# Sizes' low words, a flag asked for early, and loads planned to land later in a fused attention and expert kernel

## The chip, the cores and the metric

The kernel runs on one core of one Trainium2 chip. The metric is the device time of one execution in microseconds (us), as the median of several runs. An execution can also be profiled; the profile covers the span from the core's first to its last instruction, and the device time is a little more than that span.

## What is computed

The reference chains three layers over 1,536 tokens (2 batches of 768), with 512 features:

```python
# attention: 8 heads of 64, window n_local=96 back, first n_global=8 keys always seen, ALiBi-like bias
scores = q @ k.T / 8 - slope[h] * dist;  scores[~keep] = -1e9
a = exp(scores - max);  a = a / (sum(a) + 1e-9);  x = a @ v
# layer 2: 4 experts of width 1024, dense, mixed by normalised domain_probs
p = domain_probs / (domain_probs.sum(-1) + 1e-9)
x = sum_e p[:, e] * (relu(x @ w1[e]) @ w2[e])
# layer 3: width 2048, h * clip(h + 3, 0, 6) / 6
h = x @ w_in;  out = (h * clip(h + 3, 0, 6) / 6) @ w_out
```

`n_global` and `n_local` arrive as 64-bit integers; `w_in` and `w_out` arrive as 64-bit floats, and the kernel converts them to 32 bits itself.

## The kernel before, in words

**Two bodies.** `body(True)` is the fast path, for a window of at most 96 and at most 8 global keys. After it the kernel computes a flag from the sizes (lines 1192 to 1198), every engine loads it into a register (`values_load`, line 1199), and `body(False)`, a general path, follows under `tc.If` (line 1200). With the inputs used here the flag is 1 and all engines jump over the second body.

**Sizes.** Each 64-bit size is read as two 32-bit words. DVE casts the words (line 179), joins low and high word into one float (lines 180 to 183), and builds from it the bias table `base`: the window part (lines 184, 186), minus four times the local size (`nl4`, line 185), the global columns (line 187), the first block's table (line 188) and the global columns of the window table (line 189). The tile `fast_c` that these read is the second load on SP's queue (line 162).

**Attention.** There are 24 pairs: one pair is two heads by 256 query tokens (two blocks `qb` of 128). For each pair (`plan_pair`, line 312) PE makes scores (line 351), DVE adds the bias and finds the maximum (line 366), ACT takes the exponential and its sum (line 381), DVE adds 1e-9 and inverts the sums of both blocks in one piece (`sums`, lines 391 to 393), POOL normalises (line 401), PE transposes (line 420), ACT copies one block and DVE the other out of PSUM (lines 442 and 437), PE multiplies by the values (line 457), and ACT copies the result to `xf` (line 467). Each pair's queries and keys come by one load (line 323) and its values by another (line 330).

**Gate.** `plan_gate` (line 572) loads `domain_probs` (line 586), normalises them on DVE in nine small instructions (lines 578 to 584) and stores them to DRAM (line 589). `plan_p` (line 1107) loads each expert's row back, spread over all partitions (line 1113); the DVE product at line 984 needs it.

**Layers 2 and 3.** Forty-eight steps run over batch, expert (or layer 3) and pairs of 128-wide slices. `plan_first` makes the first product by a seven-product Strassen scheme (lines 909, 913, 916), `plan_second` the second (lines 1088, 1091, 1092). All are split into a high and a low part, so three matmuls stand for one. `plan_convert` turns the 64-bit weights into 32-bit ones in 32 rounds of seven DVE instructions and stores them to DRAM (line 747), from where line 775 reads them back for layer 3. The final step of each batch copies the output from PSUM (`finish`, line 1117) and sends it out in eight transfers (line 1146); the last two of the whole kernel (`d == KC - 1`) leave from ACT's queue, the others from SP's.

**What sets the order.** The body is not written in the order in which it is issued. Each piece of work is handed to `Plan.add` with an engine ("load" stands for SP's queue), a cost, the pieces it follows and a rank. `Plan.emit` (line 90) then plays the pieces through in its own clock: an engine that is free takes, of the pieces that are ready, the one with the lowest rank; if only a high-ranked piece is ready, it takes that one at once. A piece is ready when the pieces before it have ended, plus a lag: nothing on the same engine, `LOAD` = 2.0 behind a load on another engine, `LATENCY` = 0.25 otherwise (line 138). The order that comes out is fixed; on the chip every engine works through its own queue in that order. PE's gaps in that clock are filled with idle matmuls (line 263). Attention pair `i` has ranks near `2 * i`, layers 2 and 3 have ranks from 200 up, copies and activations that free PSUM have negative ones, and conversions 100,000 and more.

Of the kernel before, what the change touches and what calls it, by code (L numbers as in the profile page):

```python
# [17 lines left out]
ALU = mybir.AluOpType  # L18
# [3 lines left out]
P = 128  # L22
# [6 lines left out]
KC = DM // P  # L29
# [29 lines left out]
class Plan:  # L59
# [7 lines left out]
    LOAD = 2.0  # L67
# [22 lines left out]
    def emit(self):  # L90
# [16 lines left out]
        while count < n:  # L107
# [38 lines left out]
def moe_attention_kernel(ctx, tc, qk, vw, sizes, dpt, w1, w2, w_in, w_out, ident_d, fast_d, slow_d, out):  # L146
# [29 lines left out]
    ng, nl, nl4 = nv[:, 0:1], nv[:, 1:2], nv[:, 6:7]  # L176
    flag = const.tile([P, 1], I32, name="flag")
    with tc.manual_schedule(engines={mybir.EngineType.DVE}):
        nc.vector.tensor_copy(nf[:], ni[:])
        nc.vector.scalar_tensor_tensor(out=nv[:, 2:4], in0=lo, scalar=0.0, in1=hi, op0=ALU.is_lt, op1=ALU.add)  # L180
        nc.vector.scalar_tensor_tensor(
            out=nv[:, 0:2], in0=nv[:, 2:4], scalar=4294967296.0, in1=lo, op0=ALU.mult, op1=ALU.add
        )
        nc.vector.tensor_scalar(out=window, in0=rel, scalar1=nl, scalar2=NONE, op0=ALU.is_ge, op1=ALU.mult)
        nc.vector.tensor_scalar(out=nl4, in0=nl, scalar1=-4.0, scalar2=None, op0=ALU.mult)
        nc.vector.scalar_tensor_tensor(out=window, in0=rel, scalar=-4.0, in1=window, op0=ALU.mult, op1=ALU.add)
        nc.vector.tensor_scalar(out=gidx, in0=gidx, scalar1=ng, scalar2=NONE, op0=ALU.is_ge, op1=ALU.mult)
        nc.vector.scalar_tensor_tensor(out=first, in0=gidx, scalar=nl4, in1=window[:, FAR:], op0=ALU.add, op1=ALU.max)
        nc.vector.scalar_tensor_tensor(
            out=global_keys, in0=gidx[:, :NG], scalar=nl4, in1=global_keys, op0=ALU.add, op1=ALU.max  # L190
        )
# [22 lines left out]
    def t_mm(n, count):  # L214
        return count * (0.0145 + n / 2400.0)

# [4 lines left out]
    def pools(bx, fast):  # L221
# [70 lines left out]
        def plan_bias(tabs, normalised):  # L292

            made = plan.add("dve", 1.9, lambda: None, (), -2.0)
            for h in range(H):
                for kind in range(2):
                    if h == 0:
                        started[h, kind] = made
                        continue

                    def scaled(h=h, kind=kind):
# [7 lines left out]
                        "pool", 0.46 if kind else 0.3, scaled, [made, normalised[3 * (h // 2) - 3] if h > 1 else None], (h // 2 * CPB - 2) * CH + 0.1 * h + 0.5 * kind  # L309
                    )  # L310

        def plan_pair(i, c, hp, tabs, place_users, normalised, biased, outs, x_bank):
# [78 lines left out]
            def sums():  # L391
                nc.vector.tensor_scalar(out=m["sm"][:], in0=m["sm"][:], scalar1=1e-9, scalar2=None, op0=ALU.add)
                nc.vector.reciprocal(m["sm"][:], m["sm"][:])

            r = plan.add("dve", 0.4, sums, weighed, rank)
            normal = []
            for qb in range(CH):
                for j in range(2):
# [7 lines left out]
                    normal.append(plan.add("pool", 0.46 if kinds[qb] else 0.32, normalise, [r], rank))  # L406
# [793 lines left out]
    with tc.If(is_fast == 0):  # L1200
        body(False)
# [71 lines left out]
```

## Time and profile before

| | us |
|---|---|
| median of 3 runs (lowest to highest) | 848.62 (847.82 to 850.08) |
| the profiled execution | 847.26 |
| span of that execution | 845.2 |
| PE busy | 833.7 |
| DVE busy | 655.2 |
| ACT busy | 402.0 |
| POOL busy | 68.1 |

How to read it: the profiled execution took 847.26 us, of which 845.2 us are the span in which the profile sees instructions. PE is TensorE's matmuls, PEld its weight loads, DVE VectorE, ACT ScalarE, POOL GpSimd, SP SyncE. A letter q behind an engine's name means its sequencer or DMA queue. "L1146" is line 1146 of the kernel before. The granted clock of TensorE was 1.00 in all stages. A busy share near the full span says that an engine could be the bound; which wait ends last in a stage says whether it is.

### The profile page before, as it was taken

What the parts mean: (1) busy time and instruction counts of PE and PEld (TensorE: products, weight loads), DVE (VectorE), ACT (ScalarE), POOL (GpSimd) and SP (SyncE); (2) the same over time, 40 slices, a digit from 0 to 9 for tenths busy, and PEclk for the clock granted to TensorE, in tenths of its full rate; (3) what the DMA queues carried; (4) which work ended last, traced back from release to release, by engine and by line L of the source; (5) the groups of instructions that cost most, each with busy time, mean ns of one, the idle gap of its engine ahead of it and who ended that gap; (6) DMA issues with size and microseconds to landing.
All of it is one profiled execution on the core that took longest, in us unless ns stands there. A gap on an engine that the chain in (4) does not pass through costs nothing.

```text
span 845.2 us, 13646 instructions
## 1 busy us (share of the span) xinstructions
PE 833.7 (99%) x5090; PEld 763.2 (90%) x5090; DVE 655.2 (78%) x1366; ACT 402.0 (48%) x850; POOL 68.1 (8%) x131
## 2 busy tenths in 40 slices
PE   8999999999999999999999999999999999999997
PEld 6777999999999999999999999999999999999996
DVE  6999989988998977987777688689898766545442
ACT  6998643543433433543333333335666455545441
POOL 5888200000000000000000000000000000000000
PEclk9999999999999999999999999999999999999999
DMA  7873454465565565645656664744452555534302
GB/s 264 314 221 94 175 202 153 138 211 181 166 209 194 165 222 180 204 150 179 216 172 199 208 208 158 234 165 140 174 163 103 172 186 185 190 125 139 136 1 79
DMA packets 56985, 147.34 MB, mean 174 GB/s; under 512 B 6480, under 2 KB 7760, under 8 KB 56912
## 3 DMA queue, kind: packets, MB, share of 16 engines
q1 hardware_dynamic: 56480, 145.69, 52.2%
q8 instruction: 42, 0.69, 0.3%
q10 hardware_dynamic: 432, 0.71, 0.3%
q14 instruction: 31, 0.25, 0.1%
HBM read 109.66 MB, written 36.72 MB: 173 GB/s over the span
## 4 chain that ended last, share of the span: by engine, by line
PE 92%; DMA 3%; DVE 2%; POOL 1%; ACT 1%; issue 0%; SPq 0%; POOLq 0%; DVEq 0%; ACTq 0%
PE o L1091 16%; PE o L1092 15%; PE o L1088 15%; PE x_x L909 8%; PE x_x L913 8%; PE x_x L916 8%; PE w_w L913 6%; PE w_w L916 6%; PE w_w L909 6%; PE att_q L420 2%; PE att_q L351 1%; PE att_q L457 1%; DMA qkraw<-in_qk 1%; DMA w<-qkraw 1%; POOL t L401 1%; PE att_x L457 1%
## 5 line engine op out<-in xcount | busy, mean ns | idle before, releaser
L1091 PE MATMUL o<-hh,w2l 128*128 128x512 f32 (+1 forms) x768 | 259.4, 338 | 0.0
L1092 PE MATMUL o<-hl,w2h 128*128 128x512 f32 (+1 forms) x768 | 259.0, 337 | 0.0
L1088 PE MATMUL o<-hh,w2h 128*128 128x512 f32 (+1 forms) x768 | 257.8, 336 | 0.0
L933 ACT COPY snap<-x_x 128x384 f32<-128x384 f32 x144 | 68.9, 478 | 195.9 <-PE x_x L916 195.7
L946 DVE TENSOR_TENSOR c_c<-w_w,snap 128x384 f32<-128x384 f32 x144 | 80.0, 556 | 104.4 <-ACT w2h L250 58.5
L1092 PEld LDWEIGHTS o<-hl,w2h 128*128 128x128 f32 x768 | 144.4, 188 | 16.0
L1088 PEld LDWEIGHTS o<-hh,w2h 128*128 128x128 f32 x768 | 144.4, 188 | 13.4
L1091 PEld LDWEIGHTS o<-hh,w2l 128*128 128x128 f32 x768 | 144.5, 188 | 12.7
L909 PE MATMUL x_x<-xoh,w1h 128*128 128x384 f32 x384 | 129.7, 338 | 0.1
L916 PE MATMUL x_x<-xoh,w1l 128*128 128x384 f32 x384 | 129.0, 336 | 0.0
L913 PE MATMUL x_x<-xol,w1h 128*128 128x384 f32 x384 | 128.9, 336 | 0.0
L913 PE MATMUL w_w<-xol,w1h 128*128 128x384 f32 x288 | 97.1, 337 | 0.0
L909 PE MATMUL w_w<-xoh,w1h 128*128 128x384 f32 x288 | 97.0, 337 | 0.0
L916 PE MATMUL w_w<-xoh,w1l 128*128 128x384 f32 x288 | 96.8, 336 | 0.0
L250 ACT CAST w2h<-wr 128x1024 fp32r<-128x1024 f32 x48 | 50.4, 1050 | 61.2 <-PE o L1092 59.1
L909 PEld LDWEIGHTS x_x<-xoh,w1h 128*128 128x128 f32 x384 | 72.3, 188 | 3.2 <-issue 0.6
L913 PEld LDWEIGHTS x_x<-xol,w1h 128*128 128x128 f32 x384 | 72.3, 188 | 2.0
L1015 ACT CAST hh<-c_c 128x384 fp32r<-128x384 f32 x96 | 49.4, 514 | 48.3 <-DVE c_c L984 47.8
L916 PEld LDWEIGHTS x_x<-xoh,w1l 128*128 128x128 f32 x384 | 72.0, 188 | 0.0
L250 ACT CAST w1h<-wr 128x512 fp32r<-128x512 f32 x96 | 46.9, 510 | 49.5 <-PE w_w L913 45.7
L255 DVE TENSOR_TENSOR w2l<-wr,w2h 128x1024 fp32r<-128x1024 f32 x48 | 58.5, 1219 | 2.3 <-ACT w2h L250 2.3
L984 DVE SCALAR_TENSOR_TENSOR c_c<-c_c,p 128x384 f32<-128x384 f32 x96 | 53.8, 561 | 3.2
(90 smaller groups left out, 1132.7 us busy)
## 6 DMA issues: line engine op xcount, KB each, us to landing
wr<-in_w SPq DMA_DIRECT2D x64, 512.0 KB, 3.9
wr<-w SPq DMA_DIRECT2D x32, 512.0 KB, 3.5
kept<-w1h SPq DMA_DIRECT2D x24, 512.0 KB, 3.0
kept<-w1l SPq DMA_DIRECT2D x24, 512.0 KB, 4.8
w1h<-kept SPq DMA_DIRECT2D x24, 512.0 KB, 3.7
w1l<-kept SPq DMA_DIRECT2D x24, 512.0 KB, 4.9
qkraw<-in_w_in SPq DMA_DIRECT2D x16, 512.0 KB, 4.3
w<-qkraw SPq DMA_DIRECT2D x32, 256.0 KB, 4.2
```

What stands on the lines that cost most here:

```text
L250: nc.scalar.copy(out_ap, src)
L255: nc.vector.tensor_tensor(out_ap, src, hi_ap.bitcast(F32), op=ALU.subtract)
L909: nc.tensor.matmul(ps_, wh[:, a, cols], xh[:, o, kc, :], start=start and kc == 0, stop=False, skip_group_check=True,)
L913: nc.tensor.matmul(ps_, wh[:, a, cols], xl[:, o, kc, :], start=False, stop=False, skip_group_check=True)
L916: nc.tensor.matmul(ps_, wl[:, a, cols], xh[:, o, kc, :], start=False, stop=last, skip_group_check=True)
L933: nc.scalar.copy(m["n", n][:], m["x"][:, :HT])
L946: nc.vector.tensor_tensor(m[name][:], m["w"][:, :HT], m["n", n][:], op=ALU.add)
L984: nc.vector.scalar_tensor_tensor(out=room_for(), in0=src(), scalar=0.0, in1=p["p"][:, cols], op0=ALU.max, op1=ALU.mult)
L1015: nc.scalar.copy(at(0), room_for())
L1088: nc.tensor.matmul(o, wh, hh, start=first and own and f == 0, stop=False, skip_group_check=True)
L1091: nc.tensor.matmul(o, wl, hh, start=False, stop=False, skip_group_check=True)
L1092: nc.tensor.matmul(o, wh, hl, start=False, stop=end, skip_group_check=True)
```

## The change

The sizes' low words alone now feed the bias table, and `nl4` moves to ScalarE; joining the words moves, with the flag, to a planned DVE piece `ask` of rank 100 behind batch 1's attention. The flag then also tests the lower side of `n_global`. The global columns of the window table become a planned piece of their own (`with_global`). Pair 0's sums are split by block. In the planner a load's result is now 2.0 away from whatever follows, another load too (`LANDING`; before, nothing was added from load to load), and a load that follows other work is 0.3 away (before 0.25). The gate's ranks rise from 9, 12, 13 to 18, 30, 31; the first row load's from 20 to 34, the second's from -1 to 100. All engines load the flag behind the first output copy of the last batch, and only the very last output transfer, not the last two, leaves from ACT's queue.

```diff
-    LOAD = 2.0
+    LOAD = 0.3
+    LANDING = 2.0
...
-                lag = 0.0 if other == engine else self.LOAD if engine == "load" else self.LATENCY
+                if other == engine != "load":
+                    lag = 0.0
+                else:
+                    lag = self.LANDING if engine == "load" else self.LOAD if other == "load" else self.LATENCY
...
+    ng_low, nl_low = nf[:, 0, 0:1], nf[:, 1, 0:1]
         nc.vector.tensor_copy(nf[:], ni[:])
-        nc.vector.scalar_tensor_tensor(out=nv[:, 2:4], in0=lo, scalar=0.0, in1=hi, op0=ALU.is_lt, op1=ALU.add)
-        nc.vector.scalar_tensor_tensor(
-            out=nv[:, 0:2], in0=nv[:, 2:4], scalar=4294967296.0, in1=lo, op0=ALU.mult, op1=ALU.add
-        )
-        nc.vector.tensor_scalar(out=window, in0=rel, scalar1=nl, scalar2=NONE, op0=ALU.is_ge, op1=ALU.mult)
-        nc.vector.tensor_scalar(out=nl4, in0=nl, scalar1=-4.0, scalar2=None, op0=ALU.mult)
+        nc.scalar.mul(nl4, nl_low, -4.0)
+        nc.vector.tensor_scalar(out=window, in0=rel, scalar1=nl_low, scalar2=NONE, op0=ALU.is_ge, op1=ALU.mult)
...
-            made = plan.add("dve", 1.9, lambda: None, (), -2.0)
+            made = plan.add("dve", 0.9, lambda: None, (), -2.0)
+            whole = plan.add("dve", 0.22, with_global, [made], 0.0)
...
-            r = plan.add("dve", 0.4, sums, weighed, rank)
+            parts = [slice(qb, qb + 1) for qb in range(CH)] if i == 0 else [slice(0, CH)]
+            summed = [
+                plan.add("dve", 0.4, lambda part=part: sums(part), weighed[2 * part.start : 2 * part.stop], rank)
+                for part in parts
+            ]
...
-                    normal.append(plan.add("pool", 0.46 if kinds[qb] else 0.32, normalise, [r], rank))
+                    normal.append(plan.add("pool", 0.46 if kinds[qb] else 0.32, normalise, [summed[qb if i == 0 else 0]], rank))
...
-            a = plan.add("load", 0.2, lambda: nc.sync.dma_start(g[:], dpt.rearrange("e (p n) -> p e n", p=P)), (), 9)
-            b = plan.add("dve", 1.4, gate, [a], 12)
+            a = plan.add("load", 0.2, lambda: nc.sync.dma_start(g[:], dpt.rearrange("e (p n) -> p e n", p=P)), (), 18)
+            b = plan.add("dve", 1.4, gate, [a], 30)
             return plan.add(
-                "load", 0.2, lambda: nc.sync.dma_start(p_dram[:].rearrange("e (p n) -> p e n", p=P), g[:]), [b], 13
+                "load", 0.2, lambda: nc.sync.dma_start(p_dram[:].rearrange("e (p n) -> p e n", p=P), g[:]), [b], 31
             )
...
-                gates[b, g] = (t, plan.add("load", 1.0, load, wait + [gate], 20.0 if b == g == 0 else -1.0), p_users)
+                gates[b, g] = (t, plan.add("load", 1.0, load, wait + [gate], 34.0 if b == g == 0 else 100.0 if b == 0 and g == 1 else -1.0), p_users)
...
+                        if last and b == B - 1 and d == part == 0:
+                            plan.add(
+                                "act", 0.6, lambda: is_fast.append(nc.values_load(flag[0:1, 0:1], min_val=0, max_val=1)),
+                                [e], -9.0,
+                            )
...
-                            end = b == B - 1 and d == KC - 1
+                            end = b == B - 1 and d == KC - 1 and part == 1
...
+                plan.add("dve", 1.2, ask, x_ready[1], 100.0)
...
-    nc.vector.tensor_scalar(out=nv[:, 4:5], in0=nl, scalar1=1.0, scalar2=None, op0=ALU.is_ge)
...
-    is_fast = nc.values_load(flag[0:1, 0:1], min_val=0, max_val=1)
-    with tc.If(is_fast == 0):
+    with tc.If(is_fast[0] == 0):
         body(False)
```

`ask` holds six DVE instructions: the two that join the words, and four that make the flag.

## Rows read from the trace of the kernel before

**Rows 1.** The page: PE's busy time, and the chain that ended last by engine.

```profile
PE 833.7 (99%) x5090; PEld 763.2 (90%) x5090; DVE 655.2 (78%) x1366; ACT 402.0 (48%) x850; POOL 68.1 (8%) x131
...
PE 92%; DMA 3%; DVE 2%; POOL 1%; ACT 1%; issue 0%; SPq 0%; POOLq 0%; DVEq 0%; ACTq 0%
```

**Rows 2.** Stages: us, busy time of PE, PEld, DVE, ACT, POOL, PEclk, DMA share, GB/s.

```profile
20.00:40.00 20.00, 18.59 (x194) 13.98 (x192) 18.21 (x76) 18.37 (x65) 16.32 (x34) 1.00 0.87 305
...
96.00:400.00 304.00, 304.00 (x1738) 283.64 (x1739) 264.93 (x482) 125.37 (x223) 0.00 (x0) 1.00 0.56 182
...
700.00:839.00 139.00, 138.76 (x793) 128.46 (x791) 69.37 (x127) 65.20 (x121) 0.00 (x0) 1.00 0.37 126
```

**Rows 3.** Timeline, PE from 20 us: matmuls that began after idle time.

```profile
20.83 0.66 PE L457 MATMUL att_x<-at,v 104*64 104x128 f32 x8 [0.52 <-DVE at L437]
22.25 1.37 PE L351 MATMUL att_q<-qkraw 64*128 64x232 f32 x8 [0.18 <-DVE mn L366]
37.45 0.89 PE L351 MATMUL att_q<-qkraw 64*128 64x128 f32 x8 [0.70 <-DMA qkraw<-in_qk]
62.30 0.63 PE L420 MATMUL att_q<-qkraw,t 128*128 128x128 f32 x4 [1.22 <-DVE at L437]
```

**Rows 4.** Timeline of the tail: DVE's last copy.

```profile
838.92 0.42 DVE L1132 COPY xf<-o 128x256 f32<-128x256 f32 x1 [1.67 <-PE o L1092]
```

**Rows 5.** Lines 747, 1146, 1199, 1200: ns min/median/max, first and last start in us.

```profile
L747 SPq DMA_DIRECT2D w<-qkraw x32: 319/326/459, 123.6 to 688.3; - x32
...
L1146 ACTq DMA_DIRECT2D out_t<-xf x2: 351/822/1294, 838.8 to 839.4; - x2
...
L1199 PEldq TENSOR_LOAD <-flag x1: 758/758/758, 837.3 to 837.3; - x1
...
L1200 SPq EVENT_SEMAPHORE  x8: 17/17/17, 840.4 to 842.8; - x8
...
L1200 SPq COMPARE_BRANCH  x1: 53/53/53, 837.7 to 837.7; - x1
...
L1200 ACTq COMPARE_BRANCH  x1: 54/54/54, 841.3 to 841.3; - x1
...
L1200 ACTq EVENT_SEMAPHORE  x1: 17/17/17, 844.0 to 844.0; - x1
```

**Rows 6.** DMA issues: KB each, median us from issue to landing.

```profile
out_t<-xf SPq DMA_DIRECT2D x7, 128.0 KB, 1.9
...
p<-p_dram SPq DMA_DIRECT2D x8, 384.0 KB, 4.8
...
out_t<-xf ACTq DMA_DIRECT2D x1, 128.0 KB, 3.2
...
p_dram<-gate SPq DMA_DIRECT2D x1, 24.0 KB, 2.6
```

**Rows 7.** Timeline of the first 24 us: the table, pair 0, and the gate.

```profile
5.42 0.34 DVE L184 TENSOR_SCALAR base<-qkraw,nv 128x232 f32<-128x232 f32 x1
...
9.13 0.17 DVE L392 TENSOR_SCALAR sm<-sm 128x4 f32<-128x4 f32 x1 [0.99 <-ACT t L381]
...
10.12 1.66 PE L420 MATMUL att_q<-qkraw,t 128*128 128x128 f32 x6 [0.46 <-POOL t L401]
...
18.06 0.37 DVE L578 TENSOR_TENSOR gate_sum<-gate 128x12 f32<-128x12 f32 x1 [0.38 <-DMA gate<-in_dpt]
...
20.09 0.68 DVE L437 COPY at<-att_q 128x512 f32<-128x512 f32 x1
```

**Rows 8.** The chain that ended last, in order of time: three of its transfers.

```profile
1.20 4.20 DMA qkraw<-in_fast
...
28.63 8.68 DMA qkraw<-in_qk
...
688.33 5.50 DMA w<-qkraw
```

**Rows 9.** Waits of SP's queue: us in total, times, longest.

```profile
SPq L1113 <- DMA p_dram<-gate: 2.1, 1, 2.1
```

More of the change, by code (lines that the diff above doesn't have):

```diff
@@ L215, in t_mm @@
         return count * (0.0145 + n / 2400.0)
+    is_fast = []
     def body(fast):
@@ L292, in plan_bias, with with_global @@
         def plan_bias(tabs, normalised):
-            made = plan.add("dve", 1.9, lambda: None, (), -2.0)
+            made = plan.add("dve", 0.9, lambda: None, (), -2.0)
+            def with_global():
+                nc.vector.scalar_tensor_tensor(
+                    out=global_keys, in0=gidx[:, :NG], scalar=nl4, in1=global_keys, op0=ALU.add, op1=ALU.max
+                )
+            whole = plan.add("dve", 0.22, with_global, [made], 0.0)
             for h in range(H):
@@ L297, in plan_bias @@
                     if h == 0:
-                        started[h, kind] = made
+                        started[h, kind] = whole if kind else made
                         continue
@@ L308, in plan_bias @@
                     started[h, kind] = plan.add(
-                        "pool", 0.46 if kind else 0.3, scaled, [made, normalised[3 * (h // 2) - 3] if h > 1 else None], (h // 2 * CPB - 2) * CH + 0.1 * h + 0.5 * kind
+                        "pool", 0.46 if kind else 0.3, scaled, [whole if kind else made, normalised[3 * (h // 2) - 3] if h > 1 else None], (h // 2 * CPB - 2) * CH + 0.1 * h + 0.5 * kind
                     )
@@ L389, in plan_pair, with sums @@
                     )
-            def sums():
-                nc.vector.tensor_scalar(out=m["sm"][:], in0=m["sm"][:], scalar1=1e-9, scalar2=None, op0=ALU.add)
-                nc.vector.reciprocal(m["sm"][:], m["sm"][:])
-            r = plan.add("dve", 0.4, sums, weighed, rank)
+            def sums(part):
+                sm = m["sm"][:, part].rearrange("p a b -> p (a b)")
+                nc.vector.tensor_scalar(out=sm, in0=sm, scalar1=1e-9, scalar2=None, op0=ALU.add)
+                nc.vector.reciprocal(sm, sm)
+            parts = [slice(qb, qb + 1) for qb in range(CH)] if i == 0 else [slice(0, CH)]
[3 more added lines that the diff above has]
+            ]
             normal = []
@@ L1149, in finish, with ask @@
                 results[b] = done
+            if fast:
+                def ask():
+                    nc.vector.scalar_tensor_tensor(
+                        out=nv[:, 2:4], in0=lo, scalar=0.0, in1=hi, op0=ALU.is_lt, op1=ALU.add
+                    )
+                    nc.vector.scalar_tensor_tensor(
+                        out=nv[:, 0:2], in0=nv[:, 2:4], scalar=4294967296.0, in1=lo, op0=ALU.mult, op1=ALU.add
+                    )
+                    nc.vector.tensor_scalar(out=nv[:, 4:5], in0=nl, scalar1=1.0, scalar2=None, op0=ALU.is_ge)
+                    nc.vector.scalar_tensor_tensor(
+                        out=nv[:, 5:6], in0=nl, scalar=float(NPREV + 1), in1=nv[:, 4:5], op0=ALU.is_le, op1=ALU.mult
+                    )
+                    nc.vector.scalar_tensor_tensor(
+                        out=nv[:, 5:6], in0=ng, scalar=-2147483648.0, in1=nv[:, 5:6], op0=ALU.is_ge, op1=ALU.mult
+                    )
+                    nc.vector.scalar_tensor_tensor(
+                        out=flag[:], in0=ng, scalar=float(NG), in1=nv[:, 5:6], op0=ALU.is_le, op1=ALU.mult
+                    )
+                plan.add("dve", 1.2, ask, x_ready[1], 100.0)
             results = {}
```

12 lines of the change are left out of this document (2 added, 10 removed).

## The prediction, made before the change was run

> **What bounds the kernel now.** I read the page first: PE is busy for 833.7 of 845.2 us, and 92% of the chain that ended last is PE [rows 1]. Busy alone would not prove a bound, so the busy time by stage comes next: from 96 to 400 us PE is busy for 304.00 of 304 us, DVE for 264.93 [rows 2]. Layers 2 and 3 give nothing back unless matmuls go, and none do. What can move is PE's idle time: at the start, in the attention stage, and behind the last matmul. The timeline of PE from 20 us shows the attention gaps: 0.52, 0.18, 0.70 and 1.22 us [rows 3]; before them lies one of 0.46 us at 10.12 [rows 7]. In the tail DVE's last copy ends at 838.92 + 0.42 = 839.34 [rows 4], but the span ends at 845.2: 5.9 us in which no engine computes. The upper bound of the whole change is thus small: 3.1 us of gaps and a part of the tail.
>
> **The tail: -1.0 us (bounds -0.5 and -1.1).** ACT issues the last two outputs. The first issue takes 351 ns, the second 1,294 ns from 839.4, so until 840.7. Then ACT loads the flag, branches at 841.3, and its next instruction comes at 844.0, which is 2.7 us behind the branch [rows 5]. The span ends 1.2 us later. After the change the flag is in the register long before, and ACT issues one output instead of two. If that takes 0.35 us, ACT branches at 839.4 + 0.4 = 839.8 and is there at 842.5, 1.5 us earlier. But SP is then last. It now issues the second-to-last output, at 838.8 for about 0.35 us, branches at 839.2, and by its own row needs 840.4 - 837.7 = 2.7 us for the jump [rows 5]: 841.9. It then walks through eight waits on transfers and as many on engines. The last three of the first eight run from the landing of the last output, 839.4 + 3.2 = 842.6 [rows 6], to 842.8 [rows 5], so about 0.07 us each; sixteen make 1.1 us, and SP is through at 843.0 where ACT was at 844.0. Hence -1.0. If the single issue still takes 1.3 us, ACT arrives at 843.4 and only 0.5 us is gained; if SP's waits overlap more, 1.1. Here the rows weigh against a rule: a 128 KB output lands in 1.9 us from SP and in 3.2 us from ACT [rows 6], so which queue issues seems to matter.
>
> The Trainium skill, "DMA: Bandwidth & Descriptors", section "Issuing engines are not separate DMA queues", says that transfers from either engine run on the same 16 DMA engines, and that issuing from several saves sequencer time alone. By it the queue that issues makes no difference to the landing, the tail would give 0.5 us, and the sum would be -1.7. The trace's 1.9 against 3.2 us speak against it, with one transfer of this size on ACT to judge by.
>
> **The flag loads themselves: 0 (0 to +0.8).** All five engines now load the flag behind the first output copy, in the middle of the last matmuls. PE's load took 758 ns from 837.3, while PE's matmuls went on until 838.9, when DVE's copy, which waited for them, began [rows 4, 5]. PE's sequencer thus runs more than 0.76 us ahead, and the load hides there; without that lead the 0.76 us would be paid whole. On SP the load sits ahead of the first outputs, on ACT between copies; neither is late until the end. SP had loaded the flag early before and does so no longer; what it had to send then was waiting for scores anyway: 0.
>
> **The table: 0 (0 to -0.2).** Two small joins leave DVE's chain, but line 184 began at 5.42 [rows 7], right behind the landing of `fast_c` at 1.20 + 4.20 = 5.40 [rows 8]. The removed work was hidden behind that load. The product for `nl4` on ACT falls into ACT's wait for pair 0. Line 189 only becomes a piece and stays in front of the first bias. A gain would need line 188 to start earlier, and that waits for lines 184 to 187.
>
> **Pair 0 by blocks: -0.3 us (bounds 0 and -0.8).** DVE waits 0.99 us at 9.13 for all four exponentials before it inverts; PE's six transposes then take 1.66 us behind a gap of 0.46 [rows 7]. With two sums the first block can be normalised while the second is still in ACT, which costs DVE two more small instructions, twice 0.17 us, inside that 0.99 us wait. Four transposes take 0.63 us where they run on [rows 3], six thus 0.95, so 0.46 + 0.71 = 1.2 us stand idle there; two thirds of it, 0.8, bound the gain, since the second block's exponentials end no earlier. But pair 1's exponentials start where they did, so PE soon waits for them instead; I take a quarter.
>
> **The gate: -0.4 us (bounds -0.7 and +1.3).** DVE starts the gate at 18.06, after a wait of 0.38 us, and gets to the next attention copy at 20.09 [rows 7]. PE pays 0.52 + 0.18 = 0.70 us for it [rows 3]. The higher ranks do not by themselves carry the gate to pair 15: a free engine takes whatever is ready, and the copy at 20.09, of pair 2 and rank 4, ran behind the gate of rank 12, so it wasn't ready when the gate was taken. I expect the gate to slip by a pair or a few. Its 2.0 us then land where DVE is 91% busy (18.21 of 20 us [rows 2]) and cost between nothing and 2.0; I take 0.3 of it back: -0.4. What is queued behind a late gate on DVE is the copy that frees PE's transposes.
>
> **Loads: -0.4 us (bounds 0 and -0.7).** SP stood still for 2.1 us in front of the first row load, until the gate's store had landed [rows 9], with attention loads behind it. The DMA share is 0.87 from 20 to 40 us [rows 2], and one load of queries issued at 28.63 took 8.68 us [rows 8]; PE waited 0.70 us for it at 37.45 [rows 3]. With `LANDING` the plan no longer puts the row load right behind the store, and two transfers of 384 KB move back in the queue. At the rate of 305 GB/s in [rows 2] one of them is 1.3 us of transfers, more than the gap; I take a little over half.
>
> **The six instructions of `ask`: 0 (0 to +1.0).** At 0.17 us each, as the small one at 9.13 [rows 7], 1.0 us on DVE behind attention, covered by 304.00 - 264.93 = 39 us of idle DVE [rows 2]. If that cover is gone, the conversions, lowest in rank, end later by as much. **Store to load, 2.0 instead of 0: -0.1.** The last conversion's store took 5.50 us from 688.33 [rows 8] with its reader right behind; planning the reader later can only take off what PE idles there: 139.00 - 138.76 = 0.24 us from 700 us on [rows 2], of which 0.1 lie behind the last matmul.
>
> **The sum.** -1.0 - 0.3 - 0.4 - 0.4 - 0.1 = -2.2 us. The profiled execution took 847.26, so 845.1 of its kind; the median stands 1.36 us above it, and 848.62 - 2.2 = 846.4 is my forecast.
>
> **Rivals.** First, *only sequencer time in the tail*: ACT's 1,294 ns issue stays although it is alone. Then the tail gives 0.5 instead of 1.0 and the time is 846.9. By the section named above of the Trainium skill's "DMA: Bandwidth & Descriptors" it would go this way. For it: no row names a cause of the long issue. Against it: it is the second of two, 0.6 us apart, and the first took 0.35 [rows 5]. Second, *given back*: a new order moves each attention gap rather than closing it, and only the tail is left, 847.6. For it speaks that DVE and ACT are 18.2 and 18.4 of 20 us busy beside PE [rows 2]. Third, *all gaps close*: with 1.1, 0.8, 0.7, 0.7 and the 1.22 us at 62.30 [rows 3] it is 848.62 - 4.5 = 844.1. Fourth, the other side, *the rows come late*: the gate does run at its rank, near pair 15, and line 984's first product is planned on a row that has not landed. The store takes 2.6 and the row load 4.8 us [rows 6], so 7.4 against 2 x 2.0 planned behind their costs of 1.2, that is 2.2 short; under load as at 28.63 [rows 8] the row takes 8.68, and it is 6.1 short. DVE then stands still, with PE's copies behind it. With 2.0 more of gate at the gap of 1.22 the price is 4.2 to 8.1, and the time -2.2 + 6 = about 852.4. It decides once the gate ends less than 8 us ahead of that product. Against it: DVE has idle moments much earlier. Fifth, *a conversion slips a round*: PE had no slack behind the store at 688.33, and a round takes (688.3 - 123.6) / 31 = 18.2 us [rows 5]: 846.4 + 18.2 = 864.6. Against it: DVE's idle time. That the change does nothing at all is excluded by the moved outputs; that it changes the order hardly at all is the second rival.
>
> **How the numbers follow.** Chances: forecast 0.38, sequencer time only 0.12, given back 0.18, all gaps 0.21, late rows 0.08, slipped round 0.03. A measurement can tell 0.3% from no change, that is 2.5 us: faster below 846.07, slower above 851.2. Faster takes the 0.21 and 0.14 of the forecast's own spread; slower the last two; the rest is the same. The range runs from 844.1, all gaps closed, to 849.3: only the tail, with the gate at its worst bound (848.62 - 1.0 + 1.3 = 848.9) and half of the flag load's. Left out are the last two rivals and the extremes.
>
> **What would show it.** Right, step by step: ACT's branch near 839.8 on the scale of before and SP's waits the last thing; PE's gaps at 10.12, 20.83 and 37.45 gone or halved; no wait of SP between the gate's store and the first row. Wrong: a TENSOR_LOAD that leaves PE idle in its last matmuls; a DVE wait on the row tile; a PE gap near 60 us that has grown beyond 1.22; a gap of microseconds near 700. The forecast as a whole falls if PE's gaps in attention sum up to more than before, or if the tail is not shorter by half a microsecond.

## The result, and the profile after

The changed kernel is slower: 853.18 us (851.04 to 854.37, 8 runs) against 848.49 us (847.82 to 850.08, 8 runs) for the kernel before, a ratio of 1.0052 with a 95% interval of 1.0043 to 1.0061, or +4.7 us. The forecast was 846.4 us with a range up to 849.3. The profiled execution took 851.04 us with a span of 849.1 us; it is the fastest of the eight and lies 2.1 us under their median. The profiled execution of the kernel before, 847.26 us, lies under all eight of its runs and 1.2 us under their median. The sums below compare these two executions and explain 3.9 of the 4.7 us.

The page of the changed kernel, PE's busy time and the chain that ended last, answers to [rows 1]:

```profile
PE 835.8 (98%) x5093; PEld 763.6 (90%) x5093; DVE 656.7 (77%) x1368; ACT 403.5 (48%) x851; POOL 68.8 (8%) x131
...
PE 94%; DVE 2%; POOL 1%; DMA 1%; ACT 0%; issue 0%; SPq 0%; DVEq 0%; ACTq 0%
```

The span grew by 3.9 us, and 2.1 of them count as busy time of PE. Nearly none of that is more work: the same matmuls are stretched. Up to 8 us behind the last score matmuls' start PE is busy for 84.35 of 89.41 us in the changed kernel and for 82.04 of 87.11 in the kernel before, so its idle time up to there is the same, 5.1 us. The 166 transposes (line 433, was 420) take 26.98 us there instead of 25.34, and three idle matmuls more are run. So the start times have to be compared. A score group is the eight matmuls of line 351 (now 358) for one pair, counted from 0. Score group 16 begins at 54.80 us where it began at 52.50, and group 23 at 81.41 where it began at 79.11: +2.30 both times, and so it stays up to about 700 us. The last matmul ends at 840.82 where it ended at 838.89, only +1.93, so 0.37 came back near 700 us. The span ends 8.24 us behind it where it ended 6.30 behind it: +1.94. The account is thus **attention +2.30, near 700 us -0.37, tail +1.94**, together +3.87. One trace against one other is not exact: tail_stall and tail_only below have the same attention, nearly that of before, and score group 23 begins 0.59 and 1.52 us later in their profiles than in that of before; in after_pad, the changed kernel with instructions added that are never executed, it begins 3.75 us later than here. The medians of the experiments have to decide.

The stages, with the columns of [rows 2]; the first stretch is wider than in [rows 2], and the kernel before stands beside it in a fence of its own:

```profile
20.00:60.00 40.00, 38.07 (x368) 27.19 (x362) 35.80 (x146) 36.48 (x128) 31.01 (x58) 1.00 0.86 278
96.00:400.00 304.00, 304.00 (x1749) 283.35 (x1749) 265.67 (x489) 126.56 (x223) 0.00 (x0) 1.00 0.56 182
700.00:841.00 141.00, 140.82 (x808) 130.72 (x806) 70.08 (x127) 66.46 (x122) 0.00 (x0) 1.00 0.36 125
```

The same first stretch of the kernel before:

```profile
20.00:60.00 40.00, 38.59 (x383) 29.28 (x380) 37.17 (x151) 38.37 (x136) 32.21 (x61) 1.00 0.85 283
```

The reader should look at ACT, the fourth busy time. Before, it worked 38.37 of these 40 us: not even PE's 38.59 left less room. After, it works 36.48, 1.89 us less. That alone proves nothing: in the profile of t_gate below ACT works 36.13 us, and the median of t_gate is that of before. PE's gaps in the timeline, which answer to [rows 3], show where to look:

```profile
23.57 0.66 PE L470 MATMUL att_x<-at,v 104*64 104x128 f32 x8 [0.37 <-DVE at L450]
25.04 1.37 PE L358 MATMUL att_q<-qkraw 64*128 64x232 f32 x8 [0.22 <-DVE mn L373]
39.74 0.41 PE L433 MATMUL att_q<-qkraw,t 128*128 128x128 f32 x2 [0.91 <-ACT at L450]
47.25 0.87 PE L433 MATMUL att_q<-qkraw,t 128*128 128x128 f32 x4 [0.38 <-POOL t L414]
64.59 0.63 PE L433 MATMUL att_q<-qkraw,t 128*128 128x128 f32 x4 [1.21 <-DVE at L450]
```

The gaps around the gate shrank from 0.52 and 0.18 to 0.37 and 0.22, the one at 37.45 is gone, and the one of 1.21 is as before. New is 0.91 us at 39.74, behind a copy on ACT. ACT's timeline there:

```profile
36.51 0.19 ACT L388 ACTIVATION_READ_ACCUMULATOR t<-t,mn 128x1 f32 x1
38.06 1.04 ACT L250 CAST w2h<-wr 128x1024 fp32r<-128x1024 f32 x1 [1.36 <-DMA wr<-in_w]
39.02 0.58 ACT L450 COPY at<-att_q 128x512 f32<-128x512 f32 x1
```

ACT stands 1.36 us for a load of raw weights, and the attention's copy, for which PE waits, stands behind that conversion in ACT's queue. Each step of layer 2 has first weights (`w1h`) and second weights (`w2h`). Counted from the start, this is the second conversion of second weights, thus step 1's; step 0's ran at 26.69. In the kernel before the two ran at 35.97 (step 0) and 45.25 (step 1), both at once:

```profile
35.97 1.03 ACT L250 CAST w2h<-wr 128x1024 fp32r<-128x1024 f32 x1
45.25 1.06 ACT L250 CAST w2h<-wr 128x1024 fp32r<-128x1024 f32 x1
```

So the new plan gives step 1's second weights to ACT at 38.06 - 1.36 = 36.7 us, 8.6 us earlier than before. ACT's other wait for weights in this stage is in both kernels, for step 0's first weights: 0.79 us before and 0.99 after.

SP's queue of the changed kernel shows when the load went out:

```profile
29.60 0.33 SPq L1126 DMA_DIRECT2D p<-p_dram  x1
30.02 0.38 SPq L330 DMA_DIRECT2D qkraw<-in_qk  x1
30.86 0.33 SPq L337 DMA_DIRECT2D v<-in_vw  x1
31.24 0.42 SPq L1126 DMA_DIRECT2D p<-p_dram  x1
33.17 0.89 SPq L788 DMA_DIRECT2D wr<-in_w  x2
```

The two rows of the gate, before at 22.8 and 24.1 us, now go out directly ahead of the two loads with step 1's weights, of which the second weights come first. But SP did not send the first of them late because of the rows alone. It had issued the second row by 31.7 us and then stood for the buffer, until GpSimd's fourth sum of step 0's weights had read it, at 33.1 us (SP's waits, the columns of [rows 9]):

```profile
SPq L788 <- POOL wsum L845: 1.4, 1, 1.4
```

Before, step 0's second weights went out at 25.6 us, step 1's first at 28.2 and its second at 38.3. The views of DMA issues, one for each moment, give the time to landing: those of 25.6 and 28.2 us before,

```profile
wr<-in_w SPq DMA_DIRECT2D x1, 512.0 KB, 8.8
...
wr<-in_w SPq DMA_DIRECT2D x1, 512.0 KB, 8.3
```

and the pair of after:

```profile
wr<-in_w SPq DMA_DIRECT2D x2, 512.0 KB, 5.3
```

The transfers themselves were slower before. They were only early enough: 25.6 + 8.8 = 34.4, ahead of the conversion at 35.97, and 28.2 + 8.3 = 36.5, ahead of that of step 1's first weights at 39.55. After, step 1's first weights go out at 33.6 and are converted at 39.49, as soon as they have landed; its second weights go out 5.1 us earlier than before, but ACT's turn for them comes 8.6 us earlier. What was lost is the lead.

In the tail, the rows of the branch (line 1232, was 1200) and of the outputs (line 1164) answer to [rows 5]. First the part up to 844.3 us, then from there on, then the outputs:

```profile
L1232 SPq COMPARE_BRANCH  x1: 45/45/45, 841.1 to 841.1; - x1
L1232 ACTq COMPARE_BRANCH  x1: 54/54/54, 841.7 to 841.7; - x1
L1232 SPq EVENT_SEMAPHORE  x1: 17/17/17, 844.2 to 844.2; - x1
...
L1232 SPq EVENT_SEMAPHORE  x8: 17/17/17, 846.7 to 847.2; - x8
L1232 ACTq EVENT_SEMAPHORE  x2: 17/17/17, 844.5 to 844.6; - x2
```

```profile
L1164 ACTq DMA_DIRECT2D out_t<-xf x1: 357/357/357, 841.3 to 841.3; - x1
```

ACT did what was forecast: one issue of 357 ns, branch at 841.7, next instruction at 844.5. SP's jump takes 3.1 us where 2.7 were forecast, and it executes one wait at 844.2. Its next wait is at 846.7: **2.5 us in which SP executes nothing**. From there the eight waits go by at 0.07 us each, so what they wait for had come before.

### The profile page after: what moved, and what is told of

The parts are those of the page before. It is cut to its first block, busy times and chain, and to the rows that moved or that the text cites. A ratio compares the mean times of both kernels' runs of the same rounds, so it can differ in the third digit from the quotient of the medians.

```text
span 849.1 us, 13689 instructions
## 1 busy us (share of the span) xinstructions
PE 835.8 (98%) x5093; PEld 763.6 (90%) x5093; DVE 656.7 (77%) x1368; ACT 403.5 (48%) x851; POOL 68.8 (8%) x131
## 4 chain that ended last, share of the span: by engine, by line
PE 94%; DVE 2%; POOL 1%; DMA 1%; ACT 0%; issue 0%; SPq 0%; DVEq 0%; ACTq 0%
PE o L1104 16%; PE o L1105 16%; PE o L1101 16%; PE x_x L922 8%; PE x_x L926 8%; PE x_x L929 8%; PE w_w L926 6%; PE w_w L929 6%; PE w_w L922 6%; PE att_q L433 2%; PE att_q L358 1%; PE att_q L470 1%; POOL t L414 1%; PE att_x L470 1%; DMA wr<-in_w 1%; DMA qkraw<-in_fast 0%
## 5 line engine op out<-in xcount | busy, mean ns | idle before, releaser
L922 PEld LDWEIGHTS w_w<-xoh,w1h 128*128 128x128 f32 x288 | 54.1, 188 | 2.3 <-issue 0.3
```

The lines of the kernel that those rows point to most:

```text
L922: nc.tensor.matmul(ps_, wh[:, a, cols], xh[:, o, kc, :], start=start and kc == 0, stop=False, skip_group_check=True,)
```

## Experiments

In all of these, lines put into `body(False)` stand in the branch that this input does not take; Drains there are never executed and only move the place where an engine's jump lands. Ratios are to the kernel before on the same chip, with 95% intervals. What a kernel undoes is the change's edit of that name, as in the diff.

| run | median us | before us | ratio |
|---|---|---|---|
| attn_only | 850.55 | 848.23 | 1.0029 (1.0013 to 1.0044) |
| after_pad | 851.59 | 848.23 | 1.0030 (1.0018 to 1.0042) |
| tail_only | 848.24 | 848.23 | 0.9998 (0.9987 to 1.0010) |
| tail_stall | 850.97 | 848.23 | 1.0029 (1.0020 to 1.0039) |
| t_early | 852.06 | 848.86 | 1.0037 (1.0023 to 1.0051) |
| t_gate | 849.02 | 848.86 | 1.0001 (0.9992 to 1.0011) |
| t_lag | 852.86 | 848.86 | 1.0051 (1.0035 to 1.0068) |
| t_sums | 850.44 | 848.86 | 1.0017 (1.0007 to 1.0026) |
| rows_behind | 848.76 | 849.39 | 0.9989 (0.9979 to 0.9998) |
| rows_late | 849.27 | 849.39 | 0.9994 (0.9986 to 1.0003) |
| best_rb | 848.28 | 849.39 | 0.9989 (0.9980 to 0.9997) |
| best_all | 848.31 | 849.39 | 0.9987 (0.9979 to 0.9996) |
| pad_again | 850.50 | 848.70 | 1.0020 (1.0009 to 1.0031) |
| after_fill | 850.34 | 848.70 | 1.0019 (1.0010 to 1.0029) |

**attn_only: the change without its tail.**

```diff
-                        if last and b == B - 1 and d == part == 0:
-                            plan.add(
...
-                            end = b == B - 1 and d == KC - 1 and part == 1
+                            end = b == B - 1 and d == KC - 1
...
+    is_fast.append(nc.values_load(flag[0:1, 0:1], min_val=0, max_val=1))
     with tc.If(is_fast[0] == 0):
+        for _ in range(16):
+            nc.sync.drain()
         body(False)
```

Expected:

> The change without its tail: the flag is read behind the body as before and both last outputs are issued on ScalarE. 16 Drain instructions are put into the branch that is not taken, so that SP's jump lands well inside a block of instructions. Theory (the change loses twice, in the attention's first 53 us and in the tail): the last matmul ends at 840.8 as in the changed kernel (before 838.9), the tail is that of before, 6.3 us behind it, so the span is 847.1 and the time 850.4, ratio 1.0022 (1.0015 to 1.003). Rival (the whole loss is in the tail): span 845.2, time 848.5, ratio 1.000.

Measured: 850.55, +2.3 us. In the profile ACT waits 1.82 us for the weights, the last matmul ends at 841.72, and the tail is 6.61 us. The rival is out: the attention loses by itself.

**tail_only and tail_stall: the tail on the kernel before, and its stall brought back by Drains.** Both take the flag's three operations to the end of the first VectorE block, load the flag behind the first output copy and set `end` as the change does; tail_stall adds

```diff
     with tc.If(is_fast[0] == 0):
+        for _ in range(21):
+            nc.sync.drain()
         body(False)
```

Expected of tail_only:

> The kernel before with the change's tail alone: flag's three operations at the end of the first VectorE block, the flag's loads behind the first output copy, one last output on ScalarE. Theory: without the stalled fetch the changed tail is worth a little, its end would lie 8.28 - 2.48 = 5.8 us behind the last matmul where before it was 6.29: time 848.0, ratio 0.9994 (0.9985 to 1.0003). Rival (the chain of waits on SP and the jump of 2.7 to 4.1 us bound the end whatever is issued ahead, so the early flag is worth nothing): 848.5, ratio 1.000; that the early flag itself costs: 850.5, ratio 1.0024.

and of tail_stall:

> As tail_only, with 21 Drain instructions in the branch that is not taken, so that SP's jump lands at the same place (instruction 1871 of SP) as in the changed kernel. Theory (second fetch): a gap of 2.4 us appears between SP's first and second wait behind the jump, and the time is 2.4 us over tail_only, about 850.4, ratio 1.0023. Rival (the gap in the changed kernel had another cause): no gap, time as tail_only.

Measured: 848.24 and 850.97, so 2.7 us for instructions that are never executed. The waits of SP behind the jump, tail_only first (line 1206), then tail_stall up to and from 843.1 us:

```profile
L1206 SPq EVENT_SEMAPHORE  x9: 17/17/17, 844.1 to 844.7; - x9
```

```profile
L1206 SPq EVENT_SEMAPHORE  x9: 17/17/17, 843.0 to 846.0; - x9
...
L1206 SPq EVENT_SEMAPHORE  x8: 17/17/17, 845.4 to 846.0; - x8
```

Nine waits in 0.6 us, and then the same nine in 3.0 us with 2.4 us behind the first. The tail is 5.86 us against 7.95. So the early flag and the single output on ACT together save 0.44 us (6.30 - 5.86). Other traces say the same: the tail is 5.85 to 6.05 us in the six kernels that have both and no stall, and 6.30 to 6.73 in the five that have the tail of before and no pause on ACT (t_early, t_gate and t_sums have one). The median of tail_only shows none of it; its three operations in the head put score group 3 back by 0.60 us in the profile (12.30 against 11.70), which would cancel it.

**after_pad: the stall taken from the changed kernel.**

```diff
     with tc.If(is_fast[0] == 0):
+        for _ in range(8):
+            nc.sync.drain()
         body(False)
```

Expected:

> The changed kernel with 8 Drain instructions on SP inside the branch that is not taken: nothing of it is executed, but SP's jump lands 8 instructions further on. Theory (the 2.48 us between SP's first and second wait behind the jump are a second fetch of instructions, since the jump lands on the last instruction of a fetched block): the gap shrinks to under 0.3 us, the span is 849.1 - 2.4 = 846.7, and the time 2.4 us under the changed kernel's (850.8 against its median of 853.2, ratio 1.0027 to before; 848.6 against its best run). Rival (SP waits for something real there, a landing or another engine): gap and time as in the changed kernel, ratio 1.005.

Measured: 851.59, ratio 1.0030 where the changed kernel has 1.0052, so about 1.9 us less; the same kernel on another chip (pad_again) has 1.0020, 2.7 us less. The nine waits follow one another and the tail is 5.85 us:

```profile
L1232 SPq EVENT_SEMAPHORE  x9: 17/17/17, 848.0 to 848.6; - x9
```

The gap went with the landing place of the jump. SP lands on its instruction 1871 in the changed kernel and in tail_stall, and stands; it lands 8 further on in after_pad and 21 earlier in tail_only, and does not. In the changed kernel's last 9 us the profile counts eight transfers on an instruction queue, 0.07 MB, thus some 8 KB each:

```profile
q14 instruction: 8, 0.07, 2.1%
```

The Trainium skill, "Runtime: NRT & Kernel Launch", section "Instruction fetch mechanics", says that instructions are fetched in blocks, one ahead in sequence, and that a taken branch out of the window has to wait for the fetch of its target. The traces agree on the jump, 2.6 to 3.5 us from branch to next instruction on SP and ACT in these kernels, and add what the section does not have: SP executes one instruction behind the jump and then none for 2.4 to 2.5 us. That this is a second fetch, because the target is the last instruction of a block, is a reading that fits; no row shows where a block ends. ACT showed a like pause in t_sums, 1.95 us between its semaphore wait at 846.26 and its Drain at 848.21:

```profile
L1299 ACTq DRAIN  x2: 8/72/135, 846.0 to 848.2; - x2
L1299 ACTq EVENT_SEMAPHORE  x2: 17/17/17, 846.3 to 848.8; - x2
```

**t_gate, t_lag, t_sums: one edit of the plan set back at a time**, each on attn_only with 24 Drains. t_gate restores the ranks 9, 12, 13, 20 and -1, t_lag the old line for the lag, t_sums `parts = [slice(0, CH)]` for pair 0 as well. Expected, in this order:

> As attn_only, with the gate's and the gate rows' old ranks (9, 12, 13, 20 and -1). In the built program the conversion of step 1's second weights then stands three copies later on ScalarE, behind the first weights'. Theory (what costs is that conversion's place, waiting for a late load): no wait over 0.4 us on ScalarE, time +0.0 to +0.7 over before. Rival (the late gate as such costs nothing and the loss is the pair split, so the old ranks change nothing): +2.3.

> As attn_only, with the plan's lags as before (a load pays 2.0 behind it and 0.25 ahead of it). In the built program the conversion of step 1's second weights stays where the change put it, and the fourth sum too. Theory: the wait of 1.4 to 2.7 us stays, time +2.0 to +2.6 over before; the new lag has no part in the loss. Rival (the new lag sends loads out late): +0.5 or less.

> As attn_only, with pair 0's sums undivided. In the built program the first weight load then follows the gate's load directly and the four sums stand together on GpSimd. Theory: as in t_early the wait is gone, time -0.3 to +0.6 over before. Rival (the gate's later ranks cost by themselves): +1.5 to +2.5.

Measured: +0.2, +4.0 and +1.6 us. The lag has no part in the loss: t_lag keeps it all, with an ACT wait of 2.39 us. The old ranks take all of it away, although ACT still waits twice in the profile, and score group 23 begins 2.08 us later than in the profile of before. By the traces alone t_gate would not be cured; its median is. Its span also ends about 1 us later, behind a pause of 1.9 us on ACT at the end:

```profile
28.52 1.05 ACT L250 CAST w2h<-wr 128x1024 fp32r<-128x1024 f32 x1 [1.63 <-DMA wr<-in_w]
42.08 0.62 ACT L250 CAST w1h<-wr 128x512 fp32r<-128x512 f32 x1 [1.15 <-DMA wr<-in_w]
```

So "no wait over 0.4 us" was wrong, the time was right. In t_sums the wait for step 1's weights is 0.46 us, near what was expected; its +1.6 lies over the range, and 1.95 us of its tail are ACT's pause above. Its attention is thus near that of before, but this is subtraction, not a run.

**t_early: the buffer of the weights freed earlier.** The late load waits for the buffer that GpSimd's fourth sum reads (32.4 to 33.1 us, behind four pieces of normalising and four of the bias tables); the edit moves that sum up:

```diff
-    adder, cost, lambda n=n: sums(n), [summed] + wait_s, rank, port=True
+    adder, cost, lambda n=n: sums(n), [summed] + wait_s, -3.0 if i < 1 and n == 3 else rank, port=True
```

Expected:

> As attn_only (the change without its tail, 24 Drains in the branch not taken), with one rank changed: the fourth sum of step 0's weights on GpSimd is ranked ahead of the attention's normalising, so that it follows the third directly. Theory (the changed ranks and costs let the plan put six groups of normalising between the third and the fourth sum; the raw weights' buffer comes free at 33.1 instead of 28.2, the next load of weights lands at 38 to 39.4, and ScalarE, which the plan made to convert it there, stands still 1.4 to 2.7 us with the attention's copies behind it): the two loads go out by 32, no wait over 0.4 us on ScalarE for them, score group 12 starts at 37.5 to 38.1 (attn_only 40.7), and the time falls from attn_only's +2.3 to +0.0 to +0.6 over before: 848.2 to 848.8. Rival (the later gate and rows, or the split pair, cost the time by themselves): still +1.5 to +2.5, 850 to 851.

Measured: 852.06, +3.2. A plain miss. About 1 us of it is again a pause of ACT at the end (the tail is 7.46 us), and in this profile the granted clock was 0.50 from 44 to 46 us; what is left is no better than attn_only. The sum moved to 28.2 us as meant, but the load still stands behind the rows in SP's queue, and what ACT now converts first waits longer. SP's timeline, then ACT's:

```profile
30.52 0.33 SPq L1126 DMA_DIRECT2D p<-p_dram  x1
30.93 0.38 SPq L330 DMA_DIRECT2D qkraw<-in_qk  x1
31.41 0.38 SPq L337 DMA_DIRECT2D v<-in_vw  x1
31.84 0.42 SPq L1126 DMA_DIRECT2D p<-p_dram  x1
32.44 1.67 SPq L788 DMA_DIRECT2D wr<-in_w  x2
```

```profile
39.18 0.93 ACT L250 CAST w1h<-wr 128x512 fp32r<-128x512 f32 x2 [3.25 <-DMA wr<-in_w]
```

The load, now with step 1's first weights, went out at 32.44 and took 6.7 us. GpSimd's sum was not what held it: the sum ended at 29.0, while SP stood until 30.5 for the gate's store in front of the first row and sent the second at 31.8. That changed the theory.

**rows_behind: the rows behind the weights.** t_early, and the two rows are made to follow step 1's two loads in the plan; 12 Drains in the branch not taken move ACT's landing place too:

```diff
+                    if i == 1:
+                        raws.append(raws_in[k][0])
...
-... plan.add("load", 1.0, load, wait + [gate], 34.0 ...
+... plan.add("load", 1.0, load, wait + [gate] + (raws if b == 0 and g < 2 else []), 34.0 ...
```

Expected:

> As t_early (gate late, fourth sum right behind the third, tail of before), and the first two rows of the gate are planned behind step 1's two loads of weights instead of directly ahead of them; 24 Drains on SP and 12 on ScalarE in the branch not taken keep both jumps clear of a block's end. Theory (what costs in the attention is that two rows of 384 KB each were put into SP's queue directly ahead of two loads of 512 KB that ScalarE is about to convert; in t_early those went out at 32.4 and landed 6.8 us later): the first load goes out by 30 and lands by 36, ScalarE waits under 0.5 us for it (t_early 3.25, attn_only 1.82), time -0.4 to +0.6 over before. Rival (the late gate or the split pair cost by themselves): +2 to +3 as t_early.

Measured: 848.76, -0.6 us against before, and some 3.8 us from t_early by their differences to before; 1.0 of these are the tail, 6.46 us instead of 7.46, which ACT's Drains can account for. The first load goes out at 32.86, later than expected, but in this execution the head is 1.1 us late (score group 3 at 12.80), and it lands in 4.6 us. SP's timeline, then ACT's:

```profile
32.86 0.38 SPq L789 DMA_DIRECT2D wr<-in_w  x1
...
42.14 0.43 SPq L1129 DMA_DIRECT2D p<-p_dram  x1
```

```profile
37.51 0.93 ACT L250 CAST w1h<-wr 128x512 fp32r<-128x512 f32 x2 [0.76 <-DMA wr<-in_w]
```

ACT's wait falls from 3.25 to 0.76 us; that is over the 0.5 expected. Counted from score group 3, the load goes out 1.0 us earlier than in t_early, and it lands 2.1 us faster, with the rows' bytes no longer beside it. The gate is as late as in the changed kernel and pair 0 as split, so neither costs by itself. The rows' edit without the earlier sum was not run.

**rows_late: the rows late, the gate early.** t_gate, with ranks 34 and 100 for the rows.

Expected:

> As t_gate (gate's load, arithmetic and store at their old ranks, tail of before), but the two rows keep the change's ranks 34 and 100, so that they stand together directly ahead of one load of step 1's weights; Drains as in rows_behind. ScalarE converts those weights only after two more copies than in the changed kernel. Theory (rows ahead of a load cost only where ScalarE's order makes it wait for the landing): -0.7 to +0.5 over before. Rival (the rows' bytes at 25 to 30 us fill the DMA engines and cost wherever the conversions stand): +1 to +2.5.

Measured: -0.1 us, as the theory has it. The rows go out at 27.6 and 28.1 us, directly ahead of one load, and by the median cost nothing. Late rows alone are harmless too. Its profile alone would not say so: ACT stands 2.10 us there for step 0's second weights, PE 1.86 behind it, and the granted clock is 0.50 from 32 to 34 us.

Over all kernels one number goes with the medians: ACT's wait for step 1's weights. It is 1.36 to 3.25 us in the profiles of the seven that lose in the attention (the changed kernel, attn_only, after_pad, pad_again, after_fill, t_lag and t_early) and at most 1.15 in those of all others, with t_sums among them, whose loss lies in its tail.

**pad_again and after_fill: the clock.** In after_pad's profile PE stood 2.23 us behind a wait of 2.70 us on ACT, and TensorE's granted clock was 0.62 from 40 to 42 us, 0.50, its level of 1.2 GHz, from 42 to 46, and 0.67 from 46 to 48 (columns as in [rows 2], the clock third from the end):

```profile
42.00:44.00 2.00, 2.00 (x16) 1.43 (x16) 0.15 (x1) 1.85 (x9) 0.00 (x0) 0.50 0.66 262
44.00:46.00 2.00, 2.00 (x16) 1.43 (x12) 0.00 (x0) 0.84 (x4) 0.00 (x0) 0.50 0.54 164
```

Score group 12 came 1.55 us later than in the changed kernel's profile, and group 13 already 3.58 us later. The clock fell in the profiles of t_early, t_lag and rows_late as well, around PE gaps of 1.62, 2.88 and 1.86 us. Such a fall could be the 2.1 us between the profile of the changed kernel and its median. after_fill is after_pad with

```diff
+    if i == 9 and qb == 0 and spare_bank:
+        for _ in range(10):
+            nc.tensor.matmul(spare_bank[0][:, 0:192], idle[:, 0:P], idle[:], start=True, stop=True)
```

ahead of the transposes that wait.

Expected of pad_again:

> after_pad once more, as the control of after_fill on the same chip. Both theories: 849.7 to 853.3 as in after_pad, spread over 3.5 us, +2.5 over before; in a profile in which ScalarE waits over 2 us for the weights, PE's gap behind it is over 1.6 us and the granted clock falls to 0.50 for some us.

and of after_fill:

> after_pad with ten more matmuls of 192 columns on the idle tile in PE's queue, directly ahead of the two transposes that wait for ScalarE's late copy (pair 9's first turn). They cost PE about 1.0 us at full clock inside a gap of 0.91 to 2.23 us. Theory (the upper part of the changed kernel's spread comes from the granted clock, which fell to 0.50 behind PE gaps of 1.62 to 2.88 us and stayed at 1.00 behind gaps of up to 1.35 us): the gap shrinks by 0.9, the clock stays at 1.00 in the stretch from 38 to 50 us, the median falls by 0.8 to 1.8 us under pad_again and no run lies above 852.0. Rival (the spread is the landing of the weights alone): median as pad_again or up to 0.2 more, with the same highest runs.

Measured: 850.50 and 850.34, no difference, with one run of after_fill at 853.41. The theory fails as put. In pad_again's profile PE stood 2.10 us at the same place and the clock stayed at 1.00. A long gap is thus not always followed by a lower clock, and how often the clock fell in the changed kernel's eight runs stays open.

**best_rb and best_all: what is left of the change.** best_rb is the changed kernel with rows_behind's two edits; best_all sets ranks, lags, sums and the table's cost back and keeps the rest. Both have 24 Drains on SP and 12 on ACT in the branch not taken.

Expected of best_rb:

> The changed kernel with rows_behind's two edits in the attention, its own early flag and one output on ScalarE, and 24 and 12 Drains in the branch not taken. Theory: attention -0.2 to +0.4, load of the third matrix near 700 us -0.4, tail 5.85 instead of 6.30, -0.45: time 847.6 to 848.6, ratio 0.9988 (0.998 to 0.9998). Rival (rows_behind doesn't cure the attention): +1 to +2, ratio 1.0018.

and of best_all:

> The changed kernel with everything that shapes the plan of the attention set back (ranks of gate and rows, lags, pair 0's sums, cost of the table): the words, the deferred key table, the early flag and one output on ScalarE stay, and 24 and 12 Drains in the branch not taken. Theory: the attention is that of before, the tail 5.85 instead of 6.30: -0.3 to -0.7, ratio 0.9994. Rival (the kept edits in the head or the early flag cost): +0.3 or more.

Measured: -1.1 us each. Both lie under the kernel before with intervals that leave out 1, by 0.25 to 1.8 us. This gain rests on one chip, whose runs of the kernel before are the slowest of four (848.23 to 849.39). rows_behind, without the changed tail, has the same ratio there, so no median shows what the tail gives back. What best_rb does show is that the changed kernel, with both causes taken out, is no slower than the kernel before. In best_rb ACT works 38.12 of the 40 us and the tail is 6.05 us; the late gate, the split pair and the later lag do no harm there:

```profile
20.00:60.00 40.00, 38.31 (x375) 28.77 (x373) 36.53 (x153) 38.12 (x132) 31.32 (x61) 1.00 0.87 282
```

That best_rb and best_all are equal says that the later gate and the split pair bring nothing measurable either.

## Why the prediction was wrong

**The tail, -1.0 us: wrong in sign, +1.94.** The terms for ACT held: its single issue took 357 ns and it was through before SP. The rival "only sequencer time" falls with that issue. The first half of the step for SP held too: SP branches 0.3 us behind the last matmul, as forecast. What failed is "SP is through at 843.0": the jump took 3.1 us instead of 2.7, and behind its first wait came 2.48 us that no row of before shows. Without them the tail is 5.86 (tail_only), -0.44 instead of -1.0; the jump of 3.25 us there, where the sum had 2.7, is what is missing. The cause was not the early flag but the place where SP's jump lands: tail_only has the flag and no stall, and tail_stall brings the stall back with Drains. "Which queue issues seems to matter" was a wrong reading: 128 KB from SP took 3.8 us and 256 KB 3.1 beside ACT's 128 KB in 3.0, so the trace agrees with the section of the Trainium skill named in the prediction, on issuing engines. It decided nothing, since all of these had landed before SP's second wait.

**Loads, -0.4 us with bounds 0 and -0.7: the bound that excluded a loss failed.** The working said that two transfers of 384 KB "move back in the queue" and priced what they leave. It did not ask what they are put in front of, two loads of 512 KB that ACT converts next, nor what else a plan with new ranks moves: ACT's turn for step 1's second weights came 8.6 us earlier, and GpSimd's fourth sum kept their buffer until 33.1 us. The attention as a whole, forecast at -1.1 (gate, pair 0 and loads), is +2.3 us in attn_only, and the loss is gone in rows_behind, which undoes the rows' place and the late sum together. The earlier sum alone cures nothing (t_early); how the loss divides between buffer, queue and bytes stays open. The step's own fact held: SP's wait for the gate's store fell from 2.1 to 1.1 us [rows 9], and PE's 0.70 us at 37.45 [rows 3] went away. ACT, quoted at 18.4 of 20 us in a rival, was the engine to look at.

**The gate, -0.4 us: nearly nothing.** It slipped from 18.06 to 20.8 us, "by a pair or a few" as the step had it, and PE pays 0.37 + 0.22 where it paid 0.52 + 0.18: 0.1 less. **Pair 0, -0.3 us: came and went.** Score group 3 starts 0.24 us earlier, at 11.46, and group 5 at 15.35 where it started at 15.34; "PE soon waits" took all of it, not three quarters. **The flag's loads and the table, 0 each: right.** PE's last matmuls run on through the load. **The lag, -0.1: not shown.** The changed kernel gains 0.37 us near 700 us, but t_lag, with the old lags, gains 0.39 there. **`ask`, 0: right**; no wait on it shows.

**The rivals.** "The rows come late" gave 852.4 us, near the 853.18 measured, but by a mechanism that did not happen: line 984's product (now 997) waits for PE alone, never for a row. "Given back" had the kind right, that a new order moves gaps, and the sign wrong. No conversion slipped a round. How the changed kernel's runs come to spread over 3.3 us, with the profiled one lowest, no experiment settles; landing times of the same pair of loads from 5.3 (changed kernel) to 6.7 us (after_pad) and falls of the clock in four traces are both there.

## What to carry to other kernels

When transfers move in a queue, price them by what stands behind them at the new place, and by which busy engine reads that next; a load may be slow and cost nothing if it goes out early, as 8.8 us did here. In a planned order, look for the engine with the least idle time in the stage, not on the page, and for what the new order makes it wait for; not every wait there is paid, as rows_late shows. Look at the spread of the profiled executions too: the traces of tail_only and tail_stall, alike up to the end, differ by 0.9 us in the attention. And before a change of a microsecond is judged, look where a jump at the end lands: 21 instructions that were never executed cost 2.7 us.

## What the hardware showed that was not expected

From a branch to the next instruction these programs take 2.6 to 3.5 us on SP and ACT and 3.5 to 4.2 us on PE. At one landing place SP stood 2.4 to 2.5 us more, and ACT in t_sums 1.95 us. Most of the feed-forward stage ran like a clock: from 150 to 400 us the shift of a matmul against the trace of before stayed within 0.02 us in every one of these kernels, so the differences came from the attention, from steps of at most 0.6 us between 400 and 710 us, and from the tail. The second of two outputs that ACT issues 0.55 us apart took 1.26 to 1.55 us to issue in the eight kernels here that have two, a lone one 0.36. The granted clock fell to 0.50, the 1.2 GHz level, for some microseconds around PE gaps of 1.62, 1.86, 2.23 and 2.88 us, each in another kernel, and stayed at 1.00 around one of 2.10 us, at the place where the gap of 2.23 had been.
